# Gathers of the next group issued in pairs, each pair tied to a step of the group in front

## The chip, the cores and the metric

The kernel runs on one core of one Trainium2 chip. The metric is the device time of one execution in microseconds (us). Three timed runs of the kernel before took 781.81, 782.08 and 783.7 us, median 782.08. Engines are named as the profile names them: PE (TensorE, matmuls), ACT (ScalarE), DVE (VectorE), POOL (GpSimd), SP (SyncE, which issues most plain DMAs).

## The reference

Three layers follow each other on 2304 tokens of 512 numbers: a windowed attention (window 64), a dense layer of 2048 hidden units, and a layer of 8 experts where each token goes to the one expert with the greatest gate logit.

```python
x = attention(q, k, v)                       # 4 x 576 tokens, 8 heads of 64
h = x @ w_in;  x = softplus(h) @ w_out       # 512 -> 2048 -> 512
e_idx = argmax(x @ w_gate + modality_bias[modality_id], axis=1)
for e in range(8):                           # 512 -> 1024 -> 512, per expert
    mask = e_idx == e
    h = np.maximum(x[mask] @ w1[e], 0.0)
    out[mask] = gate_w[mask, None] * (h @ w2[e])
```

The change touches the expert layer alone, and nothing that it computes.

## The kernel before

**Stages.** Attention and the dense layer run in blocks of 384 tokens until about 515 us; their result is stored in DRAM as `x2s`, and a table `meta` in DRAM gets a row for every token, sorted by expert. Then the experts: three single tiles of 128 tokens, called `("e", 0)` to `("e", 2)`, then five groups (`NTRI = 5`) of three tiles (`TPB = 3`) each, one more single tile, and at the end conditional single tiles. Every group is of one expert; its tiles are named by the pair (group, tile).

**How a tile is fetched.** `places` (L684) has SP load two small pieces of the table (`mt`, `mg`) and POOL compute row numbers (`pieces`, L691). `gather` (L694) allocates `gx` (tag `xo`, three buffers) and issues four indirect DMAs on POOL (L701), each 128 rows of 512 bytes. `x_turn` (L717) transposes `gx` on DVE (L720), casts it on ACT (L731, the high part) and takes the difference on DVE (L92, the low part `x3l`).

**How a group is computed.** A group has eight steps (`KF = 8`). `t1(g, f)` (L741) issues 12 matmuls of 384 columns into `ph` (two buffers, L748 to L750), then ACT takes the Relu (`g3h`, L753) and DVE the remainder (`g3l`, L754), which also frees `ph`. `t2(g, f)` (L757) issues 9 matmuls of 512 columns (L766 to L768) on `g3h` and `g3l`, two steps behind `t1` (`LAG = 2`). At a group's end `put` scales on ACT (L823) and scatters each of the three tiles to `out` with one indirect DMA on POOL (L824).

**What sets the order.** The main loop (L953) asks for the gathers of group g + 1 in steps 0, 1 and 2 of group g, and for their `x_turn`s in steps 2, 4 and 6. A scheduler then fixes the order of every engine's instructions at build time; each engine runs its own list in order, and waits on semaphores for the others. Nothing but the `gx` buffers, the table rows and the place in POOL's list keeps a gather back. Groups are counted below from the first to the fifth.

Of the kernel before, what the change touches and what calls it, by code (L numbers as in the profile page):

```python
# [10 lines left out]
F32 = mybir.dt.float32  # L11
# [5 lines left out]
ALU = mybir.AluOpType  # L17
ET = mybir.EngineType
AX = mybir.AxisListType
P = 128  # L20
# [14 lines left out]
def attention_moe_moe_kernel(ctx, tc, q, k, v, w_in, w_out, modality, w_gate, mod_bias, w1, w2, out):  # L35
    nc = tc.nc
# [4 lines left out]
    N = B * S  # L41
    F = w_out.shape[0]
    E, _, F2 = w1.shape
    KD = D // P
    NF = F // P
    KF = F2 // P
# [6 lines left out]
    TPB = TB // P  # L53
# [16 lines left out]
    sb = ctx.enter_context(tc.tile_pool(name="sb", bufs=2))  # L70
# [179 lines left out]
    def wait_for(later, earlier, reason):  # L250
        tc.add_manual_dep(later.ins, earlier.ins.name, mybir.DependencyInfo(mybir.DependencyClass.Sync, mybir.DependencyReason.DATA), reason=reason)
# [28 lines left out]
    step = {}  # L280
# [95 lines left out]
    rows = cp.tile([P, NT, MR], I32, name="rows")  # L376
# [269 lines left out]
    def reg(row, s, engines, mx):  # L646
        return value(fl[0:1, row, s:s + 1], engines, mx)
# [33 lines left out]
    st = {}  # L681
    puts = []

    def places(s, row):  # L684

        mt = sb.tile([P, 4 * MR + 4], I32, name="mt", bufs=TPB)
        nc.sync.dma_start(mt[:, 0:4 * MR], meta[ds(row, P), :].rearrange("(t n) m -> t (n m)", n=4)[None].to_broadcast((4, 32, 4 * MR)))
        mg = sb.tile([P, MR], I32, name="mg", bufs=9)
        nc.sync.dma_start(mg, meta[ds(row, P), :].rearrange("(t n) m -> n t m", n=4))
        pieces = sb.tile([P, 4], I32, name="pieces", bufs=TPB + 1)  # L690
        nc.gpsimd.tensor_tensor(pieces, mt[:, 2:4 * MR:MR], quarter, ALU.add)  # L691
        st[s] = dict(mg=mg, pieces=pieces)

    def gather(s, row, rows=N, tag="xo", bufs=3):  # L694

        if s not in st:
            places(s, row)
        pieces = st[s]["pieces"]
        xr = sb.tile([P, 4, KD, 32], F32, name="gx", tag=tag, bufs=bufs)
        for c in range(4):  # L700
            g = nc.gpsimd.indirect_dma_start(  # L701
                out=xr[:, c].rearrange("p c d -> p (c d)"), out_offset=None, in_=x2s[0:rows, :].rearrange("n (r f) -> (n r) f", r=4),
                in_offset=bass.IndirectOffsetOnAxis(ap=pieces[:, c:c + 1].bitcast(U32), axis=0))
        st[s].update(xr=xr, g=g)

    def g_main(s):
        gather(s, reg(4, s, (ET.SP,), E * R - P))

    def g_row(g, t):
        if t == 0:  # L710
            st["row", g] = reg(4, g, (ET.SP,), E * R - TB)
        return st["row", g] + t * P

    def g_group(g, t):
        gather((g, t), None if (g, t) in st else g_row(g, t))

    def x_turn(s, into=None):  # L717
        xr = st[s]["xr"]
        xT = sb.tile([P, KD, 4, 32], F32, name="x2T", tag="s")
        d = nc.vector.transpose(out=xT.rearrange("p c n t -> p n c t"), in_=xr)  # L720
        if s == ("e", 0):
            wait_for(d, step["a"], "the gather may be late")
        if s == (0, 1):
            wait_for(d, step["hh"], "the gather may be late")
        xT = xT.rearrange("p c n t -> p c (n t)")
        if into is None:
            xh = sb.tile([P, KD, P], F32R, name="x2h", tag="xh")
            xl = sb.tile([P, KD, P], F32R, name="x2l", tag="xl")
        else:
            xh, xl = into  # L730
        nc.scalar.copy(xh, xT)  # L731
        diff(nc.vector, xl, xT, xh)
        st[s].update(xh=xh, xl=xl)


    def x_group(g, t):
        if t == 0:
            st["x", g] = (sb.tile([P, KD, TB], F32R, name="x3h", tag="xh"), sb.tile([P, KD, TB], F32R, name="x3l", tag="xl"))
        x_turn((g, t), [x[:, :, t * P:(t + 1) * P] for x in st["x", g]])

    def t1(g, f):  # L741
        xh, xl = st["x", g]
        wv = wt["w1"]
        sl = slice(f * P, (f + 1) * P)
        ph = ps.tile([P, TB], F32, name="ph3", tag="ph", bufs=2)
        for c in range(KD):
            hi, lo = wv[c // 2][:, c % 2, sl], wv[2 + c // 2][:, c % 2, sl]
            nc.tensor.matmul(ph, hi, xh[:, c, :], start=c == 0, stop=False)  # L748
            nc.tensor.matmul(ph, lo, xh[:, c, :], start=False, stop=False)  # L749
            nc.tensor.matmul(ph, hi, xl[:, c, :], start=False, stop=c == KD - 1)  # L750
        gh = sb.tile([P, TB], F32R, name="g3h", tag="gh", bufs=3)
        gl = sb.tile([P, TB], F32R, name="g3l", tag="gl", bufs=3)
        nc.scalar.activation(gh, ph, AF.Relu)  # L753
        nc.vector.scalar_tensor_tensor(gl, ph, 0.0, gh.bitcast(F32), ALU.max, ALU.subtract)  # L754
        G["3", g, f] = gh, gl

    def t2(g, f):  # L757
        gh, gl = G.pop(("3", g, f))
        wv = wt["w2"]
        hi, lo = wv[f // 4][:, f % 4, :], wv[2 + f // 4][:, f % 4, :]  # L760
        if f == 0:
            px["3"] = [ps.tile([P, D], F32, name=f"p3{t}", tag="px", bufs=TPB) for t in range(TPB)]
        for t in range(TPB):
            p = px["3"][t]
            sl = slice(t * P, (t + 1) * P)
            nc.tensor.matmul(p, gh[:, sl], hi, start=f == 0, stop=False)  # L766
            nc.tensor.matmul(p, gh[:, sl], lo, start=False, stop=False)  # L767
            nc.tensor.matmul(p, gl[:, sl], hi, start=False, stop=f == KF - 1)  # L768
        if f == KF - 1:
            for t in range(TPB):  # L770
                put((g, t), px["3"][t], "vr" if t == 1 else "qk")

    def change(s, split_, load_):
        n = reg(0, s, SE, 1)
        e = reg(1, s, (ET.SP,), E - 1)
        with tc.If(n != 0):
            split_()
            if s < NSTAT - 1:
                load_(e)
# [83 lines left out]
    steps = NB * NF  # L863
# [7 lines left out]
    for g in range(steps + LAG):  # L871
        b, f = divmod(g, NF)
# [29 lines left out]
        if b == last:  # L902
            if f == 6:
                alloc_raw()
                e0 = value(e0i[0:1, 0:1], (ET.SP,), E - 1)
                load1(e0)
                load2(e0)
            if f == 10:
                early_table(last * TPB)
                for i in range(NEARLY):  # L910
                    gather(("e", i), value(erow[0:1, i:i + 1], (ET.SP,), E * R - P), last * TB, *(("vr", 2) if i else ()))
            if f == 9:
                alloc1()
                split1()
            if f == 15:
                x_turn(("e", 0))
            if f == 13:
                alloc2()
                split2()
# [12 lines left out]
    for i in range(TPB):  # L932
        g_group(0, i)
# [19 lines left out]
    for i in range(NTRI * KF + LAG):  # L953
        g, f = divmod(i, KF)
        if g < NTRI:
            t1(g, f)
            if f < TPB:
                if g + 1 < NTRI:
                    g_group(g + 1, f)
                elif f == 0:  # L960
                    g_main(NTRI)
            if f in (2, 4, 6):
                if g + 1 < NTRI:
                    x_group(g + 1, f // 2 - 1)
                elif f == 6:
                    x_turn(NTRI)
            if f == KF - 1:
                change(g + 1, split1, load1)
        if i >= LAG:
            pg, pf = divmod(i - LAG, KF)  # L970
            t2(pg, pf)
            if pf == KF - 1:
                change(pg + 1, split2, load2)
# [57 lines left out]
```

## Time and profile before

| what | value |
|---|---|
| median of three runs | 782.08 us |
| profiled execution | 784.69 us |
| its span, first to last instruction | 782.9 us |
| PE, ACT, DVE, POOL busy share of the span | 93%, 45%, 56%, 30% |
| mean granted clock of PE | 0.976 |
| first matmul of the first group | 574.41 us |
| first scatter of group 1, 2, 3, 4, 5 | 614.19, 656.06, 698.69, 732.34, 762.92 us |

The profiled execution is 1.8 us longer than its span. Matmuls are pipelined and overlap in the records, so a stretch in which PE does all that it can shows 10.00 us busy in 10; a stretch below that has lost time. A wait of ACT "on remote" is one whose end the profile could put to no instruction of this core by its records.

### The profile page before, as it was taken

What the parts mean: (1) busy time and instruction counts of PE and PEld (TensorE: products, weight loads), DVE (VectorE), ACT (ScalarE), POOL (GpSimd) and SP (SyncE); (2) the same over time, 40 slices, a digit from 0 to 9 for tenths busy, and PEclk for the clock granted to TensorE, in tenths of its full rate; (3) what the DMA queues carried; (4) which work ended last, traced back from release to release, by engine and by line L of the source; (5) the groups of instructions that cost most, each with busy time, mean ns of one, the idle gap of its engine ahead of it and who ended that gap; (6) DMA issues with size and microseconds to landing.
All of it is one profiled execution on the core that took longest, in us unless ns stands there. A gap on an engine that the chain in (4) does not pass through costs nothing. (4 is left out here: it accounts for less than half of the span.)

```text
span 782.9 us, 12421 instructions
## 1 busy us (share of the span) xinstructions
PE 724.4 (93%) x4527; PEld 625.9 (80%) x4527; DVE 437.2 (56%) x1040; ACT 354.2 (45%) x835; POOL 231.7 (30%) x264
## 2 busy tenths in 40 slices
PE   5569999999999999999999999999399979699995
PEld 4458888888888888888888898988378958598984
DVE  5999996964398438843894289645131212122133
ACT  4787886455455545553555345532121202121233
POOL 2000000343233413342334223624653433423102
PEclk9999999999999999999999999999789989899999
DMA  9954445021121211221220042110441101111101
GB/s 319 302 206 153 166 155 168 22 62 61 41 70 60 69 48 55 62 68 36 74 68 29 1 161 96 26 57 17 157 168 28 59 24 53 31 41 28 40 1 44
DMA packets 42255, 65.08 MB, mean 83 GB/s; under 512 B 12797, under 2 KB 25469, under 8 KB 42056
## 3 DMA queue, kind: packets, MB, share of 16 engines
q1 hardware_dynamic: 37656, 54.45, 21.4%
q0 software_dynamic: 4528, 9.74, 3.9%
q8 instruction: 37, 0.61, 0.3%
q14 instruction: 34, 0.28, 0.1%
HBM read 54.37 MB, written 10.06 MB: 82 GB/s over the span
## 5 line engine op out<-in xcount | busy, mean ns | idle before, releaser
L287 PE MATMUL ph<-xh,W 128*128 128x384 f32 x384 | 133.9, 350 | 2.3 <-DVE mx L149 1.4
L92 POOL TENSOR_TENSOR gl<-a,gh 128x384 fp32r<-128x384 f32 x73 | 82.7, 1134 | 175.7 <-ACT gh L303 108.0
L289 PE MATMUL ph<-xh,W 128*128 128x384 f32 x384 | 131.4, 342 | 0.0
L288 PE MATMUL ph<-xl,W 128*128 128x384 f32 x384 | 131.2, 342 | 0.0
L316 PE MATMUL px<-W,gh 128*128 128x512 f32 x288 | 115.7, 402 | 0.0
L317 PE MATMUL px<-W,gh 128*128 128x512 f32 x288 | 113.7, 395 | 0.0
L318 PE MATMUL px<-W,gl 128*128 128x512 f32 x288 | 107.0, 398 | 0.0
L754 DVE SCALAR_TENSOR_TENSOR g3l<-ph,g3h 128x384 fp32r<-128x384 f32 x40 | 22.1, 556 | 128.4 <-ACT g3h L753 97.4
L298 ACT ACTIVATE a<-a 128x384 f32<-128x384 f32 x80 | 41.9, 524 | 100.4 <-DVE a L297 97.1
L297 DVE TENSOR_SCALAR a<-ph 128x384 int32<-128x384 int32 x80 | 44.3, 554 | 68.1 <-PE ph L289 61.0
L701 POOL DMA_INDIRECT gx<-x2s,pieces x76 | 74.5, 980 | 23.7 <-issue 20.6
L164 POOL TENSOR_TENSOR s<-s,sm 128x512 f32<-128x512 f32 (+1 forms) x24 | 24.9, 1036 | 184.0 <-DVE sm L159 154.5
L287 PEld LDWEIGHTS ph<-xh,W 128*128 128x128 f32 x384 | 72.9, 190 | 7.9 <-DVE a L300 2.1
L753 ACT ACTIVATE g3h<-ph 128x384 fp32r<-128x384 f32 x40 | 19.5, 491 | 131.3 <-PE ph L750 102.5
L303 ACT CAST gh<-a 128x384 fp32r<-128x384 f32 x96 | 49.3, 514 | 59.5 <-DVE a L300 54.1
L288 PEld LDWEIGHTS ph<-xl,W 128*128 128x128 f32 x384 | 72.9, 190 | 3.7 <-issue 0.3
L300 DVE SCALAR_TENSOR_TENSOR a<-ph,a 128x384 f32<-128x384 f32 x96 | 53.1, 553 | 38.4 <-ACT a L299 35.8
L289 PEld LDWEIGHTS ph<-xh,W 128*128 128x128 f32 x384 | 72.7, 189 | 0.9 <-issue 0.2
L318 PEld LDWEIGHTS px<-W,gl 128*128 128x128 f32 x288 | 53.7, 188 | 12.4 <-issue 0.9
L316 PEld LDWEIGHTS px<-W,gh 128*128 128x128 f32 x288 | 54.1, 188 | 11.0 <-issue 2.2
L317 PEld LDWEIGHTS px<-W,gh 128*128 128x128 f32 x288 | 54.3, 188 | 8.7 <-issue 0.3
L824 POOL DMA_INDIRECT out_dram<-o,mg x19 | 19.8, 1040 | 130.1 <-ACT o L823 123.3
(209 smaller groups left out, 1455.0 us busy)
## 6 DMA issues: line engine op xcount, KB each, us to landing
raw<-in_moe_w_in_dram SPq DMA_DIRECT2D x16, 512.0 KB
raw<-in_moe_w_out_dram SPq DMA_DIRECT2D x16, 512.0 KB
r<-in_moe_w_dram SPq DMA_DIRECT2D x8, 1024.0 KB
qk<-in_k_dram SPq DMA_DIRECT2D x27, 256.0 KB
vr<-in_v_dram SPq DMA_DIRECT2D x27, 256.0 KB
qk<-in_q_dram SPq DMA_DIRECT2D x30, 128.0 KB
x2s<-xr SPq DMA_DIRECT2D x15, 256.0 KB
early<-in_v_dram SPq DMA_DIRECT2D x5, 256.0 KB
```

The lines of the kernel that those rows point to most:

```text
L92: eng.tensor_tensor(out_, a, hi.bitcast(F32), ALU.subtract)
L287: nc.tensor.matmul(ph, W[f][:, 0, 0, sl], xh[:, c, :], start=c == 0, stop=False)
L288: nc.tensor.matmul(ph, W[f][:, 0, 0, sl], xl[:, c, :], start=False, stop=False)
L289: nc.tensor.matmul(ph, W[f][:, 0, 1, sl], xh[:, c, :], start=False, stop=c == KD - 1)
L297: nc.vector.tensor_scalar(a.bitcast(I32), ph.bitcast(I32), SIGN, None, ALU.bitwise_or)
L298: nc.scalar.activation(a, a, AF.Exp)
L300: step["a"] = nc.vector.scalar_tensor_tensor(a, ph, 0.0, a, ALU.max, ALU.add)
L303: nc.scalar.copy(gh, a)
L316: nc.tensor.matmul(px[b][t], gh[:, sl], W[f][:, 1, 0, :], start=f == 0, stop=False)
L317: nc.tensor.matmul(px[b][t], gh[:, sl], W[f][:, 1, 1, :], start=False, stop=False)
L318: step["mm2"] = nc.tensor.matmul(px[b][t], gl[:, sl], W[f][:, 1, 0, :], start=False, stop=f == NF - 1)
L701: g = nc.gpsimd.indirect_dma_start(out=xr[:, c].rearrange("p c d -> p (c d)"), out_offset=None, in_=x2s[0:rows, :].rearrange("n (r f) -> ( ...
```

## The change

From the second group on, the four gathers of a tile are no longer issued together. The first two belong to one step of the group in front and the last two to the next step, over six steps for three tiles, and each gather has an added dependency: it waits for the `g3l` of the step before the one in which it is asked for (for the very first pair: for the first step of the first group). The gathers of the first group, of the single tiles and of the last tile are as before.

```diff
-    def gather(s, row, rows=N, tag="xo", bufs=3):
+    def gather(s, row, rows=N, tag="xo", bufs=3, parts=range(4), after=None):
...
-        xr = sb.tile([P, 4, KD, 32], F32, name="gx", tag=tag, bufs=bufs)
-        for c in range(4):
+        if "xr" not in st[s]:
+            st[s]["xr"] = sb.tile([P, 4, KD, 32], F32, name="gx", tag=tag, bufs=bufs)
+        xr, pieces = st[s]["xr"], st[s]["pieces"]
+        for c in parts:
             g = nc.gpsimd.indirect_dma_start(
...
-        st[s].update(xr=xr, g=g)
+            if after is not None:
+                wait_for(g, after, "gathers spread over the steps")
+        st[s]["g"] = g
...
-        nc.vector.scalar_tensor_tensor(gl, ph, 0.0, gh.bitcast(F32), ALU.max, ALU.subtract)
+        step["g3", g, f] = nc.vector.scalar_tensor_tensor(gl, ph, 0.0, gh.bitcast(F32), ALU.max, ALU.subtract)
...
-            if f < TPB:
+            if f < 2 * TPB:
                 if g + 1 < NTRI:
-                    g_group(g + 1, f)
+                    g_group(g + 1, f // 2, range(2 * (f % 2), 2 * (f % 2) + 2), step["g3", g, f - 1] if f else step["g3", g - 1, KF - 1] if g else step["g3", 0, 0])
```

On POOL, around the first group, the list before has (`gx` gathers, `out_dram` scatters; the first eight are the first group's last two tiles, the scatters those of the single tiles):

```order
L701 DMA gx<-x2s,pieces 128x128 x8
L691 TENSOR_TENSOR pieces<-mt,quarter 128x4
L701 DMA gx<-x2s,pieces 128x128 x4
L691 TENSOR_TENSOR pieces<-mt,quarter 128x4
L824 DMA out_dram<-o,mg 2304x512 x2
L701 DMA gx<-x2s,pieces 128x128 x8
```

and now, at the same place:

```order
L702 DMA gx<-x2s,pieces 128x128 x8
L691 TENSOR_TENSOR pieces<-mt,quarter 128x4 x2
L827 DMA out_dram<-o,mg 2304x512 x3
L779 UNCONDITIONAL_BRANCH
L702 DMA gx<-x2s,pieces 128x128 x4
L779 UNCONDITIONAL_BRANCH
L702 DMA gx<-x2s,pieces 128x128 x8
```

The four gathers of the second group's first tile have moved from behind the first eight to behind the scatters.

On POOL, from one group's scatters (`out_dram`) to the next group's, the list before has:

```order
L824 DMA out_dram<-o,mg 2304x512 x2
L691 TENSOR_TENSOR pieces<-mt,quarter 128x4
L701 DMA gx<-x2s,pieces 128x128 x4
L776 UNCONDITIONAL_BRANCH
L691 TENSOR_TENSOR pieces<-mt,quarter 128x4
L701 DMA gx<-x2s,pieces 128x128 x4
L691 TENSOR_TENSOR pieces<-mt,quarter 128x4
L701 DMA gx<-x2s,pieces 128x128 x4
L824 DMA out_dram<-o,mg 2304x512
```

and now:

```order
L827 DMA out_dram<-o,mg 2304x512 x2
L691 TENSOR_TENSOR pieces<-mt,quarter 128x4
L702 DMA gx<-x2s,pieces 128x128 x2
L691 TENSOR_TENSOR pieces<-mt,quarter 128x4
L702 DMA gx<-x2s,pieces 128x128 x6
L779 UNCONDITIONAL_BRANCH
L691 TENSOR_TENSOR pieces<-mt,quarter 128x4
L702 DMA gx<-x2s,pieces 128x128 x4
L827 DMA out_dram<-o,mg 2304x512
```

Twelve gathers stand between the scatters of two groups in both lists; now eight of them (a second and a third tile, by pairs) stand at once behind the scatters, and the last four (the first tile of the group after) are held by steps that come late.

On DVE, in the third group from its step 2 (`g3l` of `ph3_6716`) to step 6 (`ph3_6844`), the list before has (`x2T` is the transposition of a gathered tile, `x3l` its low part):

```order
L720 STREAM_TRANSPOSE x2T_6805<-gx_6668 128x4x4x32
L754 SCALAR_TENSOR_TENSOR g3l_6730<-ph3_6716,g3h_6729 128x384
L92 TENSOR_TENSOR x3l_6745<-x2T_6805,x3h_6744 128x4x128
L754 SCALAR_TENSOR_TENSOR g3l_6776<-ph3_6762,g3h_6775 128x384
L720 STREAM_TRANSPOSE x2T_6861<-gx_6739 128x4x4x32
L92 TENSOR_TENSOR x3l_6745<-x2T_6861,x3h_6744 128x4x128
L754 SCALAR_TENSOR_TENSOR g3l_6802<-ph3_6788,g3h_6801 128x384
L754 SCALAR_TENSOR_TENSOR g3l_6832<-ph3_6818,g3h_6831 128x384
L754 SCALAR_TENSOR_TENSOR g3l_6858<-ph3_6844,g3h_6857 128x384
```

and now (step 2 is `ph3_6705`, step 6 `ph3_6844`):

```order
L723 STREAM_TRANSPOSE x2T_6733<-gx_6631 128x4x4x32
L92 TENSOR_TENSOR x3l_6732<-x2T_6733,x3h_6731 128x4x128
L757 SCALAR_TENSOR_TENSOR g3l_6719<-ph3_6705,g3h_6718 128x384
L757 SCALAR_TENSOR_TENSOR g3l_6763<-ph3_6749,g3h_6762 128x384
L723 STREAM_TRANSPOSE x2T_6803<-gx_6728 128x4x4x32
L92 TENSOR_TENSOR x3l_6732<-x2T_6803,x3h_6731 128x4x128
L757 SCALAR_TENSOR_TENSOR g3l_6791<-ph3_6777,g3h_6790 128x384
L723 STREAM_TRANSPOSE x2T_6861<-gx_6800 128x4x4x32
L757 SCALAR_TENSOR_TENSOR g3l_6830<-ph3_6816,g3h_6829 128x384
L92 TENSOR_TENSOR x3l_6732<-x2T_6861,x3h_6731 128x4x128
L757 SCALAR_TENSOR_TENSOR g3l_6858<-ph3_6844,g3h_6857 128x384
```

The third tile's transposition has moved from behind the `g3l` of step 3 to behind that of step 4, in front of the `g3l` of step 5.

## Rows read from the trace of the kernel before

**Rows 1.** The page: busy us, share of the span, instructions of each engine.

```profile
PE 724.4 (93%) x4527; PEld 625.9 (80%) x4527; DVE 437.2 (56%) x1040; ACT 354.2 (45%) x835; POOL 231.7 (30%) x264
```

**Rows 2.** Windows: busy us of PE, PEld, DVE, ACT, POOL; PEclk, DMA share, GB/s.

```profile
560.00:570.00 10.00, 3.73 (x9) 2.91 (x10) 3.62 (x6) 2.88 (x5) 5.06 (x6) 0.50 0.97 337
630.00:640.00 10.00, 5.99 (x13) 3.82 (x13) 1.67 (x3) 1.39 (x3) 2.90 (x4) 0.66 0.11 27
...
720.00:730.00 10.00, 10.00 (x53) 9.21 (x52) 1.47 (x3) 0.98 (x2) 0.00 (x0) 1.00 0.00 0
```

**Rows 3.** Waits, whole span: who waited for whom, us, times, longest.

```profile
ACT g3h L753 <- remote: 26.0, 3, 15.6
...
ACT o L823 <- remote: 15.7, 1, 15.7
...
PE p L783 <- ACT hh L809: 12.0, 1, 12.0
```

**Rows 4.** Timeline of PE, 545 to 641.

```profile
566.27 0.79 PE L783 MATMUL p<-w,hh 128*128 128x512 f32 x1 [11.97 <-ACT hh L809]
...
582.64 0.44 PE L748 MATMUL ph<-x3h,w 128*128 128x384 f32 x1 [1.75 <-DVE g3l L754]
...
624.58 0.33 PE L750 MATMUL ph<-x3l,w 128*128 128x384 f32 x1
...
630.17 0.34 PE L750 MATMUL ph<-x3l,w 128*128 128x384 f32 x1 [1.09 <-issue]
```

**Rows 5.** Timeline of ACT, 612 to 740.

```profile
636.87 0.49 ACT L753 ACTIVATE g3h<-ph 128x384 fp32r<-128x384 f32 x1 [15.58 <-remote]
...
678.86 0.87 ACT L753 ACTIVATE g3h<-ph 128x384 fp32r<-128x384 f32 x2 [10.27 <-remote]
...
712.08 0.49 ACT L753 ACTIVATE g3h<-ph 128x384 fp32r<-128x384 f32 x1 [0.16 <-remote]
```

**Rows 6.** Timeline of POOL, 540 to 783: start us, us, instruction, idle before.

```profile
557.54 0.97 POOL L701 DMA_INDIRECT gx<-x2s,pieces  x1 [0.15 <-issue]
...
561.32 0.94 POOL L701 DMA_INDIRECT gx<-x2s,pieces  x1 [0.32 <-issue]
...
578.38 0.95 POOL L701 DMA_INDIRECT gx<-x2s,pieces  x1 [0.30 <-issue]
...
614.19 1.00 POOL L824 DMA_INDIRECT out_dram<-o,mg  x1 [17.98 <-ACT o L823]
...
618.64 0.98 POOL L701 DMA_INDIRECT gx<-x2s,pieces  x1 [0.27 <-issue]
...
632.86 0.95 POOL L701 DMA_INDIRECT gx<-x2s,pieces  x1 [0.30 <-issue]
656.06 1.01 POOL L824 DMA_INDIRECT out_dram<-o,mg  x1 [22.25 <-ACT o L823]
...
660.70 0.99 POOL L701 DMA_INDIRECT gx<-x2s,pieces  x1 [0.27 <-POOL pieces L691]
...
674.94 0.94 POOL L701 DMA_INDIRECT gx<-x2s,pieces  x1 [0.30 <-issue]
698.69 1.01 POOL L824 DMA_INDIRECT out_dram<-o,mg  x1 [22.81 <-ACT o L823]
...
712.37 1.09 POOL L701 DMA_INDIRECT gx<-x2s,pieces  x1 [0.30 <-issue]
732.34 1.01 POOL L824 DMA_INDIRECT out_dram<-o,mg  x1 [18.88 <-ACT o L823]
```

**Rows 7.** Timeline of DVE, third group, its step 3.

```profile
663.40 0.56 DVE L754 SCALAR_TENSOR_TENSOR g3l<-ph,g3h 128x384 fp32r<-128x384 f32 x1 [3.00 <-ACT g3h L753]
```

**Rows 8.** Chain of waits: start us, us, what (a gather from issue to landing).

```profile
664.51 2.59 DMA gx<-x2s,pieces
```

**Rows 9.** Timeline of POOL at the end of an earlier run of 12 gathers.

```profile
513.07 0.95 POOL L701 DMA_INDIRECT gx<-x2s,pieces  x1 [0.30 <-issue]
```

**Rows 10.** Waits of PE, 485 to 545: the only one.

```profile
PE pc L552 <- DVE pos L487: 0.3, 1, 0.3
```

## What the change does to the time: the prediction

> **What bounds the kernel now.** I read the page first: PE is busy for 93% of the span [rows 1], so only PE's lost time can be won. Then the stretches: between 720 and 730 us, in the middle of a group, PE is busy 10.00 us in 10 at a clock of 1.00, but between 560 and 570 it is busy 3.73 us at 0.50, and between 630 and 640 5.99 us at 0.66, partly at 1.2 GHz in place of 2.4 [rows 2]. Those are holes in the expert stage, where POOL issues gathers.
>
> The waits name them: ACT waited 26.0 us "for remote" before `g3h`, the longest 15.6, and 15.7 us before one `o`, and PE waited 12.0 us once, for ACT [rows 3]. One core runs, so nothing is remote. What ACT lacked is seen by putting two timelines side by side: in the second group PE's matmul that ends a step's `ph` runs at 624.58 and is over at 624.91 [rows 4], but the `g3h` that needs it starts at 636.87 [rows 5]. So for some 12 us the word that `ph` was ready did not arrive. PE itself crept as well: the same matmul of the next step starts at 630.17, after 1.09 us in which the profile shows no wait [rows 4].
>
> POOL's timeline shows what else ran [rows 6]. The second group's gathers are issued without a pause from 618.64 to 633.81, twelve of them, and ACT goes on 3.1 us after the last; the third group's twelve run from 660.70 to 675.88, and ACT goes on at 678.86, 3.0 us after the last [rows 5, 6]. In the fourth group eight gathers end at 713.46, and ACT's comparable `g3h` starts at 712.08 with 0.16 us of such waiting [rows 5, 6]. Before the first group 16 run up to 562.26, and PE goes on at 566.27 [rows 4, 6]. So a long unbroken run of gathers goes with a hold-up of the other engines' signals, and it ends about 3 us after the run does; a run of eight costs little.
>
> **What the holes cost.** A group is timed from its first scatter to the next group's: 614.19 to 656.06 is 41.87 us (second group's computation), 656.06 to 698.69 is 42.63 (third), 698.69 to 732.34 is 33.65 (fourth, no hole) [rows 6]. The second loses 41.87 - 33.65 = 8.2 us and the third 42.63 - 33.65 = 9.0 us, slow clock after the hole included. In the first group PE waits 1.75 us for a `g3l` and goes on at 582.64, 3.3 us after the end of a run of eight gathers (578.38 + 0.95) [rows 4, 6].
>
> **The change part by part.** *Removed ahead of the first group.* The four gathers from 557.54 to 562.26, one every 1.26 us, go behind the scatters. If the hold-up ends with the run, ACT and PE go on 4 x 1.26 = 5.0 us sooner, at 561.2 in place of 566.27. The rest of that hole stays, because the eight gathers in front of these are the first group's and stay.
>
> *Removed in the groups.* The second and third group's runs of twelve are cut. Behind the scatters six gathers still run without a pause, since the steps they wait for are over by then: in the times of the third group, 660.70 plus 5 x 1.26 plus 0.95 gives an end at 667.95 in place of 675.88. The seventh and eighth wait for the `g3l` of step 4, so POOL pauses until ACT and DVE have gone on. That is a self-limiting order: the signals cannot be held while the run that holds them waits for one. I put 8.2 + 9.0 + 1.75 = 19.0 us on this.
>
> *Added: waits.* A group's step takes 33.65 / 8 = 4.21 us. Step 3's `g3l` starts at 663.40 [rows 7], so step 4's would start at 667.6. If the signal comes 3.0 us after the run's end it is there at 671.0; `g3h` 0.49 and `g3l` 0.56 make it 672.1. Two gathers follow, the second issued at 673.4, landing 2.59 us later [rows 8] at 676.0. DVE now has the third tile's transposition in front of the `g3l` of step 5 and stands waiting for it until then; with 0.7 for the transposition and 0.56 for `g3l`, step 5's `ph` is free at 677.3. Step 7 writes into it. Its matmuls are due three steps and half a step (one `t2`) behind step 3's end: PE ended step 3 about 0.6 us before the `g3l`, at 662.8, and 662.8 + 3.5 x 4.21 = 677.5. So the room is 0.2 us. Behind the waiting DVE instruction stands only that `g3l`; behind the waiting gathers on POOL stand the next gathers and the scatters, which nobody on PE waits for within a group.
>
> The trace before shows no such tied gather, so this wait is bounded: below 0, since step 4's signal may come as the fourth group's did, almost on time; above 9.0 us per group, the third group's whole hole, if the hold-up lasts as long as it did there: step 4's `g3l` would then end at 678.86 + 0.49 + 0.56 = 679.9, step 6, due at 662.8 + 2.5 x 4.21 = 673.3, would wait 6.6 us for it, and step 7 about 1.0 more behind the transposition, with the slow clock on top. I take 1.0 us in each of the four groups with tied gathers, 4.0 together, near the lower end, because the fourth group's eight gathers directly behind three scatters are the nearest case [rows 5, 6].
>
> *Costed at nothing.* The number of gathers, table loads and matmuls is the same. A tile is ready later, but step 0 of the next group is due 1.5 steps after step 7 begins, about 6 us behind the last transposition at 676.7 plus cast and low part, so that cover is some 5 us; if it were gone, each later us would cost one us per group. The scheduler's reordering of `t1` and `t2` in the first group moves no work.
>
> **The sum.** 5.0 + 19.0 - 4.0 = 20.0 us less. Of the profiled execution's 784.69 us that leaves 764.7; the median of the runs is 2.6 us below the profiled one, so I forecast 782.08 - 20.0 = 762.1 us, and by the wait's lower end 782.08 - 24.0 = 758.1.
>
> **Two rules weighed.** PE's matmuls stretched to more than 1 us apart while the DMA share was 0.11 [rows 2, 4]. The Trainium skill's page "SBUF — State Buffer", section "Who interferes with whom", holds that a DMA never contends with a compute engine and that "PE and ACT never wait on anyone". By that rule the holes have another cause; this trace does not agree with it on the face of it (15.58 us of ACT, ended with the gathers), unless what is held is no SBUF access, which the rule does not speak of.
> The page "DMA: Bandwidth & Descriptors", section "Rules for kernel authors", advises issuing a DMA early and waiting late. The change does the opposite; what that would cost here is worked out as the third rival.
>
> **The rivals.**
> *1. Spread too little.* Three scatters and six gathers still stand in a row, 12 us of POOL, and the small table loads of SP fall among them as before. If that still stops PE for 5 us in each of the second to fourth groups (the low half of 8.2 to 9.0), the sum is 5.0 + 19.0 - 15 = 9.0 less: 773. For it: the hold-up began within 6.3 us of the second group's first gather (624.91 against 618.64) [rows 4, 6]. Against: PE only crept later, and the fourth group had 14.8 us of scatters and gathers (698.69 to 713.46) without a hole.
> *2. Another cause.* An earlier run of twelve gathers ending at 514.0 left PE with no wait over 0.3 us [rows 9, 10], so length alone does not make a hole. If it is something in the second and third groups that the change leaves (the table loads, the conditional weight loads), and the wait before the first group ends by its own, nothing is won: 782. This is also what the rule on SBUF gives. Against: the end 3.0 and 3.1 us after the last gather, twice.
> *3. The tied gathers come late.* The hold-up stays as long as it was, and each group pays 9.0 us, through step 4's `g3l` and the DVE transposition that stands in front of step 5's: 4 x 9.0 = 36 against 24 won, 782 + 12 = 794. It decides from 24 / 4 = 6.0 us per group. For it: the room is 0.2 us. Against: with POOL idle nothing holds the signals, and the wait cannot feed itself. This is also the advice on early DMAs.
>
> **How the numbers follow.** The forecast gets 0.56 (756 to 768), rival 1 0.22 (768 to 779), rival 2 0.08, rival 3 0.11, and 0.03 is for more than 24 us won. The range leaves out rivals 2 and 3, and 755 is the lower end plus the spread of the three runs: 755 to 779. A difference under 0.3% (2.3 us) cannot be told from none here. Faster 0.56 + 0.22 + 0.03 = 0.81, same 0.08, slower 0.11.
>
> **What would show it.** Right: in the profile after, ACT's "remote" waits before `g3h` fall below some 5 us in all; the distances between first scatters are 33.6 to 35 us in the second to fourth groups; PE goes on at about 561 before the first group; POOL pauses between the sixth and seventh gather behind the scatters. Wrong: PE matmuls more than 1 us apart in the second or third group with runs of six gathers (rival 1), unchanged holes (rival 2), or PE waiting for `g3l` at step 7 while DVE stands before a transposition (rival 3).

## The result and the profile after

The changed kernel took 761.57 us (median of four runs, 760.02 to 762.68), the kernel before beside it 781.94 us (778.42 to 783.7). The ratio is 0.9757, 95% interval 0.972 to 0.9795: 20.4 us faster. The forecast was 762.1 us, 20.0 us faster. The profiled execution took 761.99 us, with a span of 760.3.

This holds where the kernel before takes 782 us. The runs of one batch were made one after another on one chip, and the four batches whose chip is on record on four different chips. In three of five batches before took 782 to 784 us, in two 752 us, and there the change moved nothing: 752.54 beside 752.49, ratio 1.0001 (0.9983 to 1.0018). Both are looked at below; this section is about the 782.

The page and the windows of the changed kernel (busy us of PE, PEld, DVE, ACT, POOL in each stretch; granted clock, DMA share, GB/s):

```profile
PE 717.7 (94%) x4527; PEld 621.5 (82%) x4527; DVE 436.6 (57%) x1040; ACT 354.6 (47%) x835; POOL 228.8 (30%) x264
```

```profile
550.00:560.00 10.00, 4.46 (x20) 3.16 (x18) 0.49 (x1) 0.00 (x0) 5.79 (x8) 0.94 0.19 47
560.00:570.00 10.00, 8.37 (x28) 6.48 (x28) 4.67 (x7) 3.62 (x6) 2.03 (x2) 0.72 0.88 308
620.00:630.00 10.00, 10.00 (x50) 8.88 (x49) 3.84 (x7) 2.86 (x6) 3.99 (x5) 1.00 0.12 29
630.00:640.00 10.00, 10.00 (x53) 9.20 (x52) 1.92 (x4) 0.99 (x3) 1.96 (x3) 1.00 0.04 13
```

In the second group PE is busy without a gap at a clock of 1.00, where before it had 5.99 us in 10 at 0.66 [rows 2]. The hole ahead of the first group is still there, shorter. POOL's timeline (start, us, instruction, idle before), from the second group's computation on:

```profile
608.82 1.02 POOL L827 DMA_INDIRECT out_dram<-o,mg  x1 [0.30 <-ACT o L826]
...
612.94 0.99 POOL L702 DMA_INDIRECT gx<-x2s,pieces  x1 [0.27 <-POOL pieces L691]
...
616.85 0.95 POOL L702 DMA_INDIRECT gx<-x2s,pieces  x1 [0.30 <-issue]
621.68 0.95 POOL L702 DMA_INDIRECT gx<-x2s,pieces  x1 [3.88 <-issue]
...
625.42 0.94 POOL L702 DMA_INDIRECT gx<-x2s,pieces  x1 [0.30 <-issue]
...
634.19 0.97 POOL L702 DMA_INDIRECT gx<-x2s,pieces  x1 [7.60 <-issue]
...
639.96 0.95 POOL L702 DMA_INDIRECT gx<-x2s,pieces  x1 [3.54 <-DVE g3l L757]
...
642.45 1.01 POOL L827 DMA_INDIRECT out_dram<-o,mg  x1 [0.31 <-ACT o L826]
...
676.11 1.01 POOL L827 DMA_INDIRECT out_dram<-o,mg  x1 [0.30 <-ACT o L826]
...
709.67 1.01 POOL L827 DMA_INDIRECT out_dram<-o,mg  x1 [11.40 <-ACT o L826]
...
740.25 0.97 POOL L827 DMA_INDIRECT out_dram<-o,mg  x1 [26.98 <-ACT o L826]
```

The run of twelve is cut into four, four, two and two. The first pause of 3.88 us ends when step 3's `g3l` is over. That step's last matmul ended at 615.45, but ACT got it late (PE, ACT and DVE timelines of the changed kernel, one row each):

```profile
615.11 0.34 PE L753 MATMUL ph<-x3l,w 128*128 128x384 f32 x1
```

```profile
619.86 0.49 ACT L756 ACTIVATE g3h<-ph 128x384 fp32r<-128x384 f32 x1 [7.78 <-PE ph L753]
```

```profile
620.38 0.56 DVE L757 SCALAR_TENSOR_TENSOR g3l<-ph,g3h 128x384 fp32r<-128x384 f32 x1 [7.50 <-ACT g3h L756]
```

So the signal is still held, for 619.86 - 615.45 = 4.4 us, until 2.1 us after the fourth gather (616.85 + 0.95); but the run is of four gathers, not of twelve, and PE has other steps' work for that long. It is the signal that is late and not ACT: in the trace's semaphore records this matmul's update stands at 619.77, 4.3 us after its end. Where the time went, from the two profiled executions (us):

| stretch | before | after | won |
|---|---|---|---|
| to the first matmul of the first group | 574.41 | 570.17 | 4.2 |
| from it to the first group's first scatter | 39.78 | 38.65 | 1.1 |
| second group | 41.87 | 33.63 | 8.2 |
| third group | 42.63 | 33.66 | 9.0 |
| fourth group | 33.65 | 33.56 | 0.1 |
| fifth group | 30.58 | 30.58 | 0.0 |
| from the last group's first scatter to the end | 19.98 | 20.05 | -0.1 |

Together 22.6 us, the difference of the spans (782.9 - 760.3).

### The profile page after: what moved, and what is told of

Its sections match the earlier page's. It is cut to its first block, busy times and chain, and to the rows that moved or that the text cites. A ratio compares the mean times of both kernels' runs of the same rounds, so it can differ in the third digit from the quotient of the medians.

```text
span 760.3 us, 12435 instructions
## 1 busy us (share of the span) xinstructions
PE 717.7 (94%) x4527; PEld 621.5 (82%) x4527; DVE 436.6 (57%) x1040; ACT 354.6 (47%) x835; POOL 228.8 (30%) x264
## 5 line engine op out<-in xcount | busy, mean ns | idle before, releaser
L702 POOL DMA_INDIRECT gx<-x2s,pieces x76 | 72.9, 959 | 71.3 <-issue 54.7
L317 PEld LDWEIGHTS px<-W,gh 128*128 128x128 f32 x288 | 54.3, 188 | 8.7 <-issue 0.3
L751 PE MATMUL ph<-x3h,w 128*128 128x384 f32 x160 | 54.3, 340 | 1.0 <-ACTq L779 0.9
```

The costliest lines, as they stand in the source:

```text
L317: nc.tensor.matmul(px[b][t], gh[:, sl], W[f][:, 1, 1, :], start=False, stop=False)
L702: g = nc.gpsimd.indirect_dma_start(out=xr[:, c].rearrange("p c d -> p (c d)"), out_offset=None, in_=x2s[0:rows, :].rearrange("n (r f) -> ( ...
```

## The experiments

The theories: *mine*, that a long unbroken run of gathers holds the other engines' signals, and that a gather tied to such a signal ends the run; the *table loads* of SP among the gathers (the second rival); and that the *pairs or places* help without the waits.

### The added wait taken out

```diff
-                    g_group(g + 1, f // 2, range(2 * (f % 2), 2 * (f % 2) + 2), step["g3", g, f - 1] if f else step["g3", g - 1, KF - 1] if g else step["g3", 0, 0])
+                    g_group(g + 1, f // 2, range(2 * (f % 2), 2 * (f % 2) + 2))
```

> The changed kernel without the added dependency. If before takes 782 us here: 778 to 784 by my theory (nothing breaks the runs of twelve gathers), 760 to 764 if asking in pairs is what helps. If before takes 752: 752, and it tells nothing apart.

Measured beside 782.89 us: 792.82 us, ratio 1.0126 (1.0068 to 1.0184), slower than before and 31 us slower than the changed kernel's 761.57 of another batch. POOL's timeline of this kernel, the ends of the second and the fourth group's run and a scatter:

```profile
615.63 0.99 POOL L702 DMA_INDIRECT gx<-x2s,pieces  x1 [0.27 <-POOL pieces L691]
...
629.84 0.94 POOL L702 DMA_INDIRECT gx<-x2s,pieces  x1 [0.30 <-issue]
...
654.72 1.01 POOL L827 DMA_INDIRECT out_dram<-o,mg  x1 [23.94 <-ACT o L826]
...
702.65 0.99 POOL L702 DMA_INDIRECT gx<-x2s,pieces  x1 [0.27 <-POOL pieces L691]
...
716.85 0.94 POOL L702 DMA_INDIRECT gx<-x2s,pieces  x1 [0.30 <-issue]
```

and its ACT and PE in the second group's run:

```profile
618.15 0.49 ACT L756 ACTIVATE g3h<-ph 128x384 fp32r<-128x384 f32 x1 [3.72 <-issue]
...
634.06 0.49 ACT L756 ACTIVATE g3h<-ph 128x384 fp32r<-128x384 f32 x1 [10.57 <-remote]
```

```profile
625.27 0.42 PE L751 MATMUL ph<-x3h,w 128*128 128x384 f32 x1
628.24 0.48 PE L752 MATMUL ph<-x3h,w 128*128 128x384 f32 x1 [2.55 <-issue]
629.67 0.48 PE L753 MATMUL ph<-x3l,w 128*128 128x384 f32 x1 [0.95 <-issue]
631.78 0.48 PE L751 MATMUL ph<-x3h,w 128*128 128x384 f32 x1 [1.63 <-issue]
```

The twelve gathers are one run again, from 615.63 to 630.78; ACT goes on 3.3 us after its end, and PE creeps, one matmul in 1.4 to 3 us. The second, third and fourth group take 43.19, 43.85 and 40.63 us. The wait, not the asking in pairs, makes the gain. It was expected that the time would be that of before; it is 10 us more. The spans of the two profiled executions differ by 7.1 us (790.0 - 782.9), and 7.0 of that (40.63 - 33.65) is the fourth group, which now has a run of twelve too, where before had eight.

### Table loads taken out of the runs

```diff
-    for i in range(TPB):
-        places((1, i), g_row(1, i))
...
+    for i in range(TPB):
+        places((1, i), g_row(1, i))
...
+            if f == 5 and g + 2 < NTRI:
+                for t in range(TPB):
+                    places((g + 2, t), g_row(g + 2, t))
```

The second group's loads go behind the first group's weights, the others five steps into the group two in front. (`mt`, `mg` and `pieces` have 6, 16 and 9 buffers in place of 3, 9 and 4.)

> The kernel before with the table loads of SP out of the runs of gathers, once more. If before takes 782 us here: by my theory the second and third group stay at 40 to 43 us and the time within 776 to 787 us; by the rival (table loads make the hold-up) groups of 33.6 us and 758 to 767 us. If before takes 752: about 757, as it did.

Measured: 783.26 beside 782.89, ratio 1.0001 (0.9968 to 1.0034). The scheduler moved gathers too: twelve stand in a row ahead of the first group, where before had 16, and 20 in it. In the second group's run one load of each table is left. The third group's is free of them; the DMA view of this kernel from 640 to 690 us, which holds that whole run:

```profile
q0 software_dynamic: 717, 1.76, 11.3%
q14 instruction: 2, 0.02, 0.1%
q8 instruction: 1, 0.02, 0.1%
```

No packet of SP's queue (`q1`) is in it, so there is no table load among these twelve gathers. POOL and ACT there:

```profile
666.10 0.99 POOL L701 DMA_INDIRECT gx<-x2s,pieces  x1 [0.15 <-issue]
...
680.13 0.95 POOL L701 DMA_INDIRECT gx<-x2s,pieces  x1 [0.30 <-issue]
```

```profile
683.49 0.88 ACT L753 ACTIVATE g3h<-ph 128x384 fp32r<-128x384 f32 x2 [9.50 <-PE ph L750]
```

ACT still waits until 2.4 us after the run. So table loads are not needed for the hold-up. Its size is another matter. Both groups were expected at 40 to 43 us, and took 39.32 and 35.76 (622.64 to 661.96 to 697.72); the third loses 35.76 - 33.65 = 2.1 us, less than the 9.0 of before, which by the expectation would mean that table loads take part. Against that, the kernel with only the second group's first tile tied, below, takes 40.25 and 35.73 us with table loads in both runs. Each of these is one execution, and at 752 us, where nothing is held, moving the loads costs 4.9 us by itself, so a part of theirs in the size of a hold is not excluded. The first group, with its run of 20 gathers (580.61 to 606.31), takes 54.3 us in place of 39.8, and the sum stayed.

### Runs of sixteen

```diff
-        for c in range(4):
+        for c in list(range(4)) * (2 if s[0] != "e" and s[1] == 1 else 1) if isinstance(s, tuple) else range(4):
```

> The kernel before with the four gathers of a group's second tile issued twice, the same rows to the same place, so that runs have up to sixteen gathers. If before takes 782 us here: the hold-ups last 4 x 1.26 = 5 us longer in the second and third group, 790 to 796 us. If before takes 752 and signals are held only beyond some length of a run: holes appear, 756 us or more. If nothing is held there at any length: 752 to 754 us, PE's signals on time, since POOL has room (16 gathers and 3 scatters take 24 of a group's 33.6 us).

Measured: 823.07 beside 782.89, ratio 1.0513 (1.0463 to 1.0563). The waits of PE in this kernel (who waited for whom: us, times, longest):

```profile
PE p L783 <- ACT hh L809: 17.3, 1, 17.3
```

Against 12.0 before [rows 3], with four gathers more in that run: 5.3 us for 4 x 1.26 = 5.0 expected, so this hole grew with the run. The second and third group take 48.18 and 47.58 us, 6.3 and 5.0 more. The total was mis-sized because I had counted two places, and the doubled gathers also lengthen the hole ahead of the first group (5.8 us later at the first scatter), the first group (12.9) and the fourth (6.5).

### Whole tiles in place of pairs

```diff
-            if f < 2 * TPB:
+            if f in (0, 2, 4):
...
-                    g_group(g + 1, f // 2, range(2 * (f % 2), 2 * (f % 2) + 2), step["g3", g, f - 1] if f else step["g3", g - 1, KF - 1] if g else step["g3", 0, 0])
+                    g_group(g + 1, f // 2, range(4), step["g3", g, f - 1] if f else step["g3", g - 1, KF - 1] if g else step["g3", 0, 0])
```

> The changed kernel with whole tiles in place of pairs, once more. If before takes 782 us here: by my theory the waits cut the runs in the second to fourth group to four gathers as the pairs do, groups 33.6 us, 759 to 765 us in all; if a pair is what lets signals through, groups of 35 us or more and 767 us or more. If before takes 752: 751, as it did.

Measured: 773.49 beside 783.77, ratio 0.9895 (0.983 to 0.9961). My expectation failed; the second, third and fourth group take 37.81, 37.82 and 38.83 us. The POOL and ACT rows show why:

```profile
608.92 0.99 POOL L702 DMA_INDIRECT gx<-x2s,pieces  x1 [0.27 <-POOL pieces L691]
...
614.17 0.97 POOL L702 DMA_INDIRECT gx<-x2s,pieces  x1 [0.27 <-issue]
...
617.95 0.94 POOL L702 DMA_INDIRECT gx<-x2s,pieces  x1 [0.30 <-issue]
```

```profile
610.67 0.49 ACT L756 ACTIVATE g3h<-ph 128x384 fp32r<-128x384 f32 x1 [3.72 <-issue]
...
621.76 0.49 ACT L756 ACTIVATE g3h<-ph 128x384 fp32r<-128x384 f32 x1 [4.89 <-remote]
```

Step 3's matmul ended 1.7 us behind the run's start here, and its signal still got through (610.24 + 0.34 on PE, `g3h` at 610.67); in the changed kernel it ended 2.5 us behind (615.45 - 612.94) and was held. Both kernels make the fifth gather wait for step 3. Here that wait was over before POOL came to it, eight gathers ran on, and step 4's signal was held for them all. So a wait ends a run only if it is for a signal that falls into that run. Pairs have a second chance, since their seventh gather waits for step 4, and at 752 us (below) they do stop there; that this is why they are better where signals are held is not shown, because there the changed kernel had stopped at the fifth.

### Only the second group's first tile tied

```diff
-        gather((g, t), None if (g, t) in st else g_row(g, t))
+        gather((g, t), None if (g, t) in st else g_row(g, t), after=step["g3", 0, 0] if (g, t) == (1, 0) else None)
```

> The kernel before with only the second group's first tile tied to the first group's first step, once more. If before takes 782 us here: the hole ahead of the first group 4 to 5 us shorter, but the first group gets a run of twelve gathers, signals held some 15 us, and loses 4 to 8 us; second and third group 40 to 43 us: 780 to 790 us. If the tie to a late signal helps by itself, without a shorter run, the first group stays below 40 us and the time falls to 776 to 778. If before takes 752: 752.

Measured: 790.89 beside 783.77, ratio 1.0092 (1.0054 to 1.013). The profiled execution took 783.39 us, 7.5 less than the median. In it the first scatter comes 5.0 us earlier (561.03, in the trace of before 566.01), as the sum had it for this part. But the tied gathers run on into the next twelve, sixteen in a row from 574.34 to 594.35, and ACT goes on 3.3 us after them:

```profile
597.60 0.49 ACT L755 ACTIVATE g3h<-ph 128x384 fp32r<-128x384 f32 x1 [15.48 <-remote]
```

and from that scatter to the first group's own are 60.31 us (561.03 to 621.34) against 48.18 before: 12.1 lost where 4 to 8 were expected. A single wait moved a run here; it did not break it. The third group (661.59 to 697.32) loses 35.73 - 33.65 = 2.1 us, and its DMA view over its run (666.2 to 681.4) has table loads:

```profile
mg<-meta SPq DMA_DIRECT2D x2, 2.0 KB
mt<-meta SPq DMA_DIRECT2D x2, 8.0 KB
```

### A tie ahead of the first group as well

```diff
-    for i in range(TPB):
+    for i in range(TPB - 1):
         g_group(0, i)
+    places((0, TPB - 1), g_row(0, TPB - 1))
...
     h_turn(("e", 2))
+    g_group(0, TPB - 1, range(4), step["hh", ("e", 2), 0])
```

(The two waits that named the third tile's last gather name the second tile's now.)

> The changed kernel with one more tie: the four gathers of the first group's third tile, the last of the run of twelve ahead of the first group, wait for the high and low part of the last single tile's first half (hh). If before takes 782 us here: that run is eight long, PE goes on at 555 to 557 us in place of 561.7, and then waits for the third tile; the first group's first matmul at 566 to 568 in place of 570.2, 757 to 760 us in all. If the late tile costs as much as the hole: 761 to 765 us. If before takes 752 and nothing is held, the tie only costs: 754 to 758 us.

Measured: 761.96 beside 783.77, ratio 0.9745 (0.9683 to 0.9808): the changed kernel's time again. Its PE:

```profile
554.69 0.50 PE L786 MATMUL p<-w,hh 128*128 128x512 f32 x1 [0.39 <-ACT hh L812]
568.56 0.69 PE L751 MATMUL ph<-x3h,w 128*128 128x384 f32 x1 [7.86 <-ACT x3h L734]
```

The hole of the hold-up is gone (PE goes on at 554.69, for 561.67 in the changed kernel), and 7.86 us of waiting for the late tile stand in its place. The last of its gathers was issued at 561.25 and the transposition started at 567.15, 5.9 us later, in a stretch in which the weight loads keep the DMA engines 0.99 busy; the 2.59 of [rows 8] were read in a quieter one. Where before takes 782 us, no version here beats the changed kernel.

### The batches in which nothing is held

In two batches the kernel before took 752 us. The changed kernel once more:

> The changed kernel once more, beside the kernel before. In the four runs just made the kernel before took 752 us and PE's signals were never held while gathers ran. My theory (the change wins only what held signals cost, 31 us of holes in the profile of before): if before takes 752 us here, no difference within 0.3% and groups of 33.6 us; if it takes 782, 762 us. If the change won its 20 us by something else (an order of PE or of the DMAs that is better by itself): 20 us faster in both cases, 732 us beside 752.

Measured: 752.54 beside 752.49, ratio 1.0001 (0.9983 to 1.0018). Four of the kernels above were run there too: without waits 751.98 and 752.17 (ratios 0.9992 and 0.9987), whole tiles 751.2 (0.9989), only the first tile tied 752.67 (1.0012), table loads moved 757.04 (1.0069, 1.0051 to 1.0087). What was expected of them was

> The changed kernel without the added dependency; the gathers are still asked for in pairs over six steps. POOL's list between the scatters of two groups then has twelve gathers with nothing that holds them back, as before. If the waits break the runs (my theory): as before, 778 to 784 us, the second and third group 40 to 43 us long, ACT waiting more than 8 us at once for a step's ph. If asking for the gathers in pairs over six steps is what helps: 760 to 764 us, groups of 33.6 us.

> The changed kernel with whole tiles in place of pairs: the four gathers of a tile are asked for in steps 0, 2 and 4 and wait for the g3l of steps 7 (of the group in front), 1 and 3. My theory (a run of gathers holds the other engines' signals, and a gather that waits for such a signal ends the run): the runs in the groups are four long, as the changed kernel's longest, groups 33.6 us, 759 to 765 us in all. If the pair matters, since four gathers at once already cost PE time: second to fourth group 35 us or more each, 767 us or more.

> The kernel before with one thing of the change: the four gathers of the second group's first tile wait for the first group's first step. My theory: the hole ahead of the first group is 4.2 us shorter (as in the changed kernel), the second and third group stay at 41 to 43 us; the first group now has a run of twelve gathers behind its scatters and loses 3 to 8 us by it: 778 to 786 us. If that hole is set by something other than the run's length (the table loads of SP): no change at any of these places, 780 to 784 us, and the first group stays below 39 us.

> The kernel before with the small table loads of SP out of the runs of gathers: those of a group are issued five steps into the group two in front, and the second group's behind the first group's weights (more buffers for the tables); the gathers are where they were. If the run's length alone holds the signals (my theory): 776 to 784 us, second and third group 40 to 43 us. If it is the table loads among the gathers (the second rival): the holes go, second and third group 33.6 us, 758 to 767 us. In between (36 to 39 us a group) both take part.

and, the second time without waits,

> The changed kernel without the added dependency, once more. If before takes 782 us here, my theory says 778 to 784 us, with the second and third group 40 to 43 us, since nothing breaks the runs of twelve; if asking in pairs is what helps, 760 to 764. If before takes 752 us: 752 again, and it tells nothing apart.

These tell the theories apart in one way only: the kernel without waits has the same run of twelve there, at the same pace, and nothing is held. Its POOL, ACT and windows:

```profile
602.97 0.99 POOL L702 DMA_INDIRECT gx<-x2s,pieces  x1 [0.27 <-POOL pieces L691]
...
617.18 0.94 POOL L702 DMA_INDIRECT gx<-x2s,pieces  x1 [0.30 <-issue]
```

```profile
605.48 0.49 ACT L756 ACTIVATE g3h<-ph 128x384 fp32r<-128x384 f32 x1 [3.72 <-PE ph L753]
...
610.66 0.48 ACT L756 ACTIVATE g3h<-ph 128x384 fp32r<-128x384 f32 x1
```

```profile
600.00:610.00 10.00, 10.00 (x52) 9.10 (x51) 1.72 (x3) 1.02 (x3) 7.74 (x10) 1.00 0.34 112
610.00:620.00 10.00, 10.00 (x51) 8.88 (x50) 3.69 (x7) 2.52 (x5) 6.31 (x8) 1.00 0.19 51
```

Twelve gathers in 15.2 us, PE busy 10.00 in 10. So a run of gathers goes with every hold-up but is not enough; something outside the kernel decides whether it comes. What that is stays open. The batches at 752 us ran on chips 1 and 5, two of those at 782 us on chips 6 and 8 (for the first, none is on record), so the chip and the time of the run changed together and no run tells them apart. A gather's row is the same (971 ns in the one, 969 in the other, both without waits). One difference can be seen in the traces: a DMA of POOL leaves 16 records of semaphore updates as it lands, 1808 for the 113 of one execution. At 752 us each of the six traces has 1802 or more of them; at 782 us each of the seven with as many DMAs has 612 to 757, records are missing already in the first 400 us, long before the experts, and their DMA view gives no median time to landing for the gathers (2.6 us at 752). Whether that is a cause of the hold-up or another effect of what causes it is not shown.

Against its own run at 752 us the changed kernel still loses 9 us where signals are held, nearly all of it ahead of the first group, whose first matmul starts at 570.17 there and at 561.89 here.

## Why the prediction was right, point by point

**The cause.** Right where before takes 782 us: the end of a hold-up follows the end of the run by 2.1 to 3.3 us in the rows shown, the hole ahead of the first group grew with the run, and without the waits the holes are back. Length is not all: runs of twelve gathers cost a group from 2.1 us (first tile tied) to 10.2 (without waits), and what else sets the size stays open. One reading was wrong. The prediction took from before's fourth group that a run of eight costs little, since ACT waited only 0.16 us for `g3h` at 712.08. But ACT stood for the tile's transposition until 711.30:

```profile
711.30 0.62 ACT L731 CAST x3h<-x2T 128x512 fp32r<-128x512 f32 x1 [5.30 <-DVE x2T L720]
```

The step's last matmul ended at 709.61, so its signal was 2.5 us late, hidden behind that wait. PE lost nothing there; in whole tiles, runs of eight cost 4.2 us a group.

**The rule weighed**, that a DMA never contends with a compute engine (the Trainium skill, "SBUF — State Buffer", "Who interferes with whom"): the batches at 752 us agree with it (PE 10.00 us busy in 10 beside twelve gathers), those at 782 do not (a matmul in 1.4 to 3 us), unless what is held there is no access to SBUF.

**Ahead of the first group, -5.0.** Measured -4.6 where PE goes on (561.67 for 566.27), -4.2 at the first group's first matmul.

**In the groups, -19.0.** Measured 8.2 + 9.0 + 1.1 = 18.3; of the 1.75 us in the first group 1.1 came. That these 1.1 are held signals is not shown: at 752 us, where nothing is held, the changed kernel takes 37.8 us for that group and the one without waits 39.8.

**The added wait, +4.0.** This term was mis-sized: it is 0. The second to fourth group take 33.63, 33.66 and 33.56 us, and PE waits for no `g3l` from 535 us on. The working had come to a room of 0.2 us and so to no wait; the 1.0 us a group was taken on top of it. The DVE instruction that I had feared did stand and wait, 4.85 us for its gathers:

```profile
628.25 0.71 DVE L723 STREAM_TRANSPOSE x2T<-gx 128x512 f32<-128x512 f32 x1 [4.85 <-DMA gx<-x2s,pieces]
628.89 0.52 DVE L757 SCALAR_TENSOR_TENSOR g3l<-ph,g3h 128x384 fp32r<-128x384 f32 x1
```

but step 5's `g3l` was over at 629.41, 14.0 us after step 3's last matmul, where the working had 14.5 (677.3 - 662.8), and step 7's first matmul followed at 630.00. The way there was another: the run stopped after four gathers, not six, because step 3's own signal was held, which I had read as on time from the `g3l` of before at 663.40. The eighth gather still started 10.0 us after that matmul (625.42 - 615.45), where the working had 10.6. In the batch at 752 us, where nothing is held, six gathers do run on behind the scatters (603.82 to 611.15) and the pause comes before the seventh, as forecast.

**The sum.** 24.0 without the wait, less 0.8 and 0.6 for the two smaller terms, is 22.6 in the profiles. The medians differ by 20.4, because the profiled run of before lay 2.8 us above its median and that of after 0.4. So the forecast hit by errors that cancel, which is luck: 4.0 too much for the wait, 1.4 too much won, and 2.3 because the profiled run of before was that much further above its median (where it was longer is not shown). The batch was luck too: in two of five batches nothing is won. The range's lower end, 755, was to be 758.1 less the spread of the three runs; that spread is 1.9 us, so 756 would have followed, and nothing hung on it.

**Its signs.** Group times and the place where PE goes on came as said. POOL's pause came after the fourth gather and not the sixth. ACT's "remote" waits did not fall below 5 us:

```profile
ACT g3h L756 <- remote: 11.7, 2, 7.1
...
ACT o L826 <- remote: 10.7, 1, 10.7
```

The holds are shorter, not gone; PE no longer pays for those in the groups.

**The rivals.** The first, spread too little, is what whole tiles do: runs of eight and 4.2 us a group. The second fell as to the table loads, but its doubt, that length alone makes no hole, was right: at 752 us none of the lengths tried does. It would have given "no change" there, and I had given that 0.08. The third did not happen.

## What to carry to other kernels

Where an engine waits for a signal whose producer is done, put its row beside the timelines of the engines off the path: if the wait ends a few microseconds after a run of software DMAs, suspect the run, and take the break out again to see whether the wait comes back. What counted here is where the run was broken, not how many gathers there were. Tie each piece to the newest signal that falls into the run itself; a wait for an older one is already over, and a single wait may only move the run. Time such a change on more than one batch and chip, since its whole worth can hang on something that the kernel does not set.

## What was not expected of the hardware

The same kernel takes 752 or 782 us by batch, with like rows for a matmul and a gather; without the waits it is 752 or 793. In the slower batches a signal of PE is held for up to 18.9 us while POOL issues gathers (with the table loads moved, a matmul of the first group ended at 591.60 and its `g3h` started at 610.47), and PE's own instructions come 1.4 to 3 us apart. A hold-up begins at no fixed point of a run: step 3's signal was held 2.5 us behind the start in the changed kernel, and got through 2.4 us behind it in the one without waits (617.71 + 0.34 on PE, the run from 615.63), where step 4's was the first to be held, 6.6 us behind. The last signal that a run holds came 1.5 us (changed kernel, fourth group: 686.54 after 685.06) to 4.2 us (table loads moved, first group: 610.47 after 606.31) after the run's end in the runs read here. One signal may get through sooner: with the table loads moved, step 4's of the second group came 0.4 us before its run's end (641.32, 641.76), and step 5's 2.5 us after it.
